# Key sums as running float32 sums instead of TensorE columns, merged masks also on GpSimd, and a new instruction order, in a four-layer attention kernel

## The chip, the cores and the metric

One core of a Trainium2 chip runs one program. The metric is device time in microseconds for one execution. The profile speaks of five engines: PE is TensorE's matmuls (PEld its weight loads), DVE is VectorE, ACT is ScalarE, POOL is GpSimd and SP is SyncE, which here only issues DMAs.

## The reference

Four attention layers in a row, each with a residual: linear attention (A), windowed softmax attention (B), A, B, on 2048 tokens of width 512, with 32 heads of 16.

```python
def _A_ref(x, wqkv, wo):                      # linear attention
    q, k, v = heads(x @ wqkv)                 # 32 heads of 16
    phi = lambda t: jnp.where(t > 0, t + 1, jnp.exp(t)) + 1e-6
    pq, pk = phi(q), phi(k)
    kv = jnp.einsum("bhsd,bhse->bhde", pk, v)
    z = jnp.einsum("bhsd->bhd", pk)           # the key sums
    num = jnp.einsum("bhqd,bhde->bhqe", pq, kv)
    den = jnp.einsum("bhqd,bhd->bhq", pq, z)[..., None] + 1e-6
    return merge(num / den) @ wo

def _B_ref(x, wqkv, wo):                      # causal window of 256
    scores = q @ k.T * 16 ** -0.5, masked to 0 <= i - j < 256
    return merge(softmax(scores) @ v) @ wo

x = x + _A_ref(_layernorm(x), A_wqkv, A_wo)
x = x + _B_ref(_layernorm(x), B_wqkv, B_wo)
x = x + _A_ref(_layernorm(x), A_wqkv, A_wo)
x = x + _B_ref(_layernorm(x), B_wqkv, B_wo)
```

## The kernel before

The 2048 tokens are 16 tiles (T) of 128. The residual stream `xres`, the normalised and transposed activations `XQ`, the keys `pk` and the values `vA` of all tiles stay in SBUF.

The program is first recorded as a graph of small steps (`Graph.add`), each with the engines it may run on, a key that once ordered it, the data it reads and writes, and its PSUM bank. `place` then reads from a packed `TABLE` the total order of all steps, the engine of each step that has a choice, and the bank of each PSUM tile. `synchronise` puts in the waits that this order needs. Each engine plays its steps in that order, so an instruction that waits holds up everything behind it on its engine. Two rules in these functions bear on GpSimd: each of its steps waits for the one before it, and a long GpSimd step waits for the last preceding wide VectorE step in the order (`WIDE`: the clamp `E1`, the normalisation `xn`, the masks `mk` and `mf`).

The stages, with the names used below:

- Keys of layer 1 (`layer_a_keys`): for each tile the layer norm (`stats`, `aggr`, `eps`, `pow`, `xn`, L367 to L371; `pow` is on GpSimd), a transpose `T` by PE or by DMA, the key projection `k` (L406), and `phi` of it: exponential `E` on ScalarE (L429), clamp `E1` (L430) and `phi` (L431) on VectorE. Then `g` (L481) adds up the Gram matrix of normalised tile and keys in four PSUM banks. When all tiles are done, `ge` (L395) copies it to SBUF and `gv` (L495) multiplies it by the value weights, which gives the key-value matrix `kv`.
- The key sums `z` of layer 1 (L504): for each tile and each quarter of the width, one matmul with the 128 x 128 keys as weights and one column of ones as data, 64 in all, added up in PSUM.
- `barrier`: `kvm` masks the key-value matrix (L523), `zs` spreads the key sums (L524), `M` multiplies by the output weights (L527), `den`, `rec`, `spread` and `pqd` make the denominators and scale the queries with their reciprocals (L543 to L563). `rec` and `pqd` are small SBUF tiles of these steps.
- The windowed layers (`middle`): per tile the linear layer's output `aout`, norm, projections `bq`, `bk`, `bv` (L406, L420) with copies `bqe`, `bke`, `bve` (L395, L591, L592), scores `s` (L638, and L679 or L682 for the far part) with exponentials `ex` (L648, L692), masks `mk` (L657, L658, L702) and `mf` (L710, L711), values `pv` (L731), division (L742, L743), a DMA transpose `oT` of the output tile and the output projection `bout`, then the residual (L574). In the first windowed layer a mask may be on VectorE or GpSimd, as `TABLE` says. In the second one, near and far masks of most tiles are merged, and this merged `mk` (L702) is a VectorE step only.
- In the second linear layer, keys and values are projected as tiles come out of the windowed layer. At its end `a_kv` adds up the key-value matrix of all tiles, and with each tile's four matmuls (L457) come its four key-sum matmuls (L460):

```python
for f in range(4):
    e.matmul(K.ps(kv)[:, fs], K.vA[:, t, fs], K.pk[:, t, fs], start=t == 0 and f == 0, stop=t == T - 1)
for f in range(4):
    m = e.matmul(K.ps(z)[:, f:f + 1], K.pk[:, t, fs], K.ones[:, 0:1], start=t == 0 and f == 0, stop=t == T - 1)
```

The table `oT` has room for two transposed output tiles, used in turn.

## Time and profile before

| | |
|---|---|
| time, median of 3 runs | 408.69 us (408.23 to 409.67) |
| profiled execution, own time | 409.79 us |
| its span | 408.1 us |
| granted TensorE clock, mean | 0.999 |

The profile follows that one execution. Busy times of engines overlap. The chain that ended last goes back from the last instruction, at each step to what released it. An idle time in square brackets is that of the engine just before the group, with what ended it.

### The profile page before, as it was taken

What the parts mean: (1) busy time and instruction counts of PE and PEld (TensorE: products, weight loads), DVE (VectorE), ACT (ScalarE), POOL (GpSimd) and SP (SyncE); (2) the same over time, 40 slices, a digit from 0 to 9 for tenths busy, and PEclk for the clock granted to TensorE, in tenths of its full rate; (3) what the DMA queues carried; (4) which work ended last, traced back from release to release, by engine and by line L of the source; (5) the groups of instructions that cost most, each with busy time, mean ns of one, the idle gap of its engine ahead of it and who ended that gap; (6) DMA issues with size and microseconds to landing.
All of it is one profiled execution on the core that took longest, in us unless ns stands there. A gap on an engine that the chain in (4) does not pass through costs nothing.

```text
span 408.1 us, 18068 instructions
## 1 busy us (share of the span) xinstructions
PE 386.1 (95%) x7922; PEld 262.9 (64%) x7997; DVE 333.4 (82%) x758; ACT 341.3 (84%) x441; POOL 151.6 (37%) x246
## 2 busy tenths in 40 slices
PE   8999999998999999999999999999999999899895
PEld 4544776766575566565665777676767766576663
DVE  5998898979998898887857789988798768776774
ACT  3465569998999999999998345999899999999992
POOL 3555624443464455451742223132313223030351
PEclk9999999999999999999999999999999999999999
DMA  7934316333263535343232000345214433345352
GB/s 247 243 65 103 106 41 136 106 77 85 69 95 81 120 83 113 75 116 93 60 72 41 16 2 27 98 100 126 65 46 121 109 89 74 74 111 115 83 146 81
DMA packets 67654, 37.88 MB, mean 93 GB/s; under 512 B 48248, under 2 KB 62712, under 8 KB 67576
## 3 DMA queue, kind: packets, MB, share of 16 engines
q1 hardware_dynamic: 67184, 35.67, 36.6%
q8 instruction: 63, 1.03, 1.1%
q0 software_dynamic: 384, 1.05, 0.7%
q14 instruction: 15, 0.12, 0.1%
q10 hardware_dynamic: 8, 0.00, 0.0%
HBM read 6.29 MB, written 2.10 MB: 21 GB/s over the span
## 4 chain that ended last, share of the span: by engine, by line
PE 69%; ACT 12%; DVE 9%; DMA 5%; issue 2%; SPq 1%; ACTq 0%
PE ps L406 22%; PE ps L420 18%; PE ps L731 14%; ACT pb L648 9%; PE ps L638 7%; DMA xres<-in_A_x_dram 2%; PE ps L682 2%; DMA pb<-in_B_wqkv_dram 2%; DVE stats L367 1%; DVE vp L431 1%; PE ps L679 1%; ACT vp L648 1%; PE ps L457 1%; ACT pb L692 1%; DVE o L743 1%
## 5 line engine op out<-in xcount | busy, mean ns | idle before, releaser
L648 ACT ACTIVATE pb<-ps 128x1024 bf16<-128x1024 f32 (+3 forms) x224 | 198.4, 973 | 8.1 <-PE ps L638 6.6
L731 PEld LDWEIGHTS ps<-vB,pb 128*128 128x128 bf16 x2560 | 77.7, 96 | 11.2 <-issue 5.0
L731 PE MATMUL ps<-vB,pb 128*128 128x34 bf16 x2560 | 83.1, 177 | 1.0 <-issue 0.8
L420 PE MATMUL ps<-xT,wBp 128*128 128x128 bf16 x1024 | 68.8, 219 | 0.3 <-ACT pb L648 0.3
L420 PEld LDWEIGHTS ps<-xT,wBp 128*128 128x128 bf16 x1024 | 58.7, 98 | 10.6 <-issue 4.6
L710 POOL TENSOR_SCALAR_AFFINE_SELECT pb<-pb 128x1024 bf16<-128x1024 bf16 x35 | 40.4, 1155 | 64.0 <-DVE pb L702 37.2
L429 ACT ACTIVATE tE<-ps 128x512 bf16<-128x512 f32 x64 | 37.8, 605 | 24.6 <-PE ps L406 15.0
L692 ACT ACTIVATE pb<-ps 128x1024 bf16<-128x1024 f32 x50 | 49.3, 1052 | 2.1 <-PE ps L682 1.0
L657 POOL TENSOR_SCALAR_AFFINE_SELECT pb<-pb 128x512 bf16<-128x512 bf16 x50 | 33.7, 674 | 45.0 <-ACT pb L648 18.1
L574 DVE TENSOR_TENSOR xres<-ps,xres 128x512 bf16<-128x512 f32 x63 | 42.8, 682 | 9.3 <-PE ps L406 9.0
L638 PE MATMUL ps<-XQ,kB 32*128 32x256 bf16 (+2 forms) x1024 | 48.1, 262 | 2.2 <-ACT pb L648 0.8
L370 POOL TENSOR_TENSOR rs<-ve,negh 128x1 f32<-128x1 f32 x64 | 37.0, 578 | 32.1 <-DVE ve L369 27.5
L406 PE MATMUL ps<-wA,XQ 128*128 128x512 bf16 x179 | 45.9, 379 | 2.8 <-DMA XQ<-vp 0.8
L367 DVE BATCH_NORM_STATS2 stats<-xres 128x6 f32<-128x512 bf16 x64 | 43.7, 685 | 3.1 <-DMA xres<-in_A_x_dram 2.3
L420 PE MATMUL ps<-XQ,wA 128*128 128x128 bf16 x512 | 35.4, 219 | 0.1
L369 POOL TENSOR_SCALAR ve<-mv 128x1 f32<-128x1 f32 x45 | 11.3, 252 | 63.2 <-DVE mv L368 61.1
L420 PEld LDWEIGHTS ps<-XQ,wA 128*128 128x128 bf16 x512 | 30.5, 98 | 5.9 <-issue 0.7
L638 PEld LDWEIGHTS ps<-XQ,kB 32*128 32x128 bf16 x1024 | 15.4, 92 | 27.6 <-ACT pb L648 9.3
L742 DVE RECIPROCAL rc<-ps 128x16 f32<-128x16 f32 x64 | 16.1, 252 | 20.2 <-PE ps L731 19.7
L406 PE MATMUL ps<-wBv,xT 128*128 128x512 bf16 x108 | 30.1, 380 | 2.4 <-issue 1.3
L406 PE MATMUL ps<-wBo,oT 128*128 128x512 bf16 x103 | 28.5, 380 | 3.0 <-issue 1.8
L406 PE MATMUL ps<-M,XQ 128*128 128x512 bf16 x114 | 29.7, 380 | 1.3 <-issue 0.6
(116 smaller groups left out, 562.0 us busy)
## 6 DMA issues: line engine op xcount, KB each, us to landing
vB<-vS SPq DMA_DIRECT2D x64, 136.0 KB, 2.6
kB<-vp SPq DMA_DIRECT2D x64, 128.0 KB, 2.4
wA<-in_A_wqkv_dram SPq DMA_DIRECT2D x3, 512.0 KB, 5.2
xres<-in_A_x_dram SPq DMA_DIRECT2D x2, 512.0 KB, 4.8
pb<-in_B_wqkv_dram SPq DMA_DIRECT2D x1, 1024.0 KB, 8.6
out_dram<-xres POOLq DMA_DIRECT2D x8, 128.0 KB, 2.7
out_dram<-xres SPq DMA_DIRECT2D x7, 128.0 KB, 2.9
xres<-in_A_x_dram SPq DMA_DIRECT2D x3, 256.0 KB, 4.9
```

Source lines behind the costliest of these rows:

```text
L367: self.on("DVE", "stats", lambda e: e.bn_stats(K.stats[:, t, :], K.xres[:, t, :]), key, dve(512), rd=[("xres", t)], wr=[("stats", t)])
L370: self.pow = self.on("POOL", "pow", lambda e: e.tensor_tensor(K.rs[:, t, :], K.ve[:, t, :], K.negh[:], ALU.pow), key + 0.03, (640, 690), r ...
L406: m = e.matmul(K.ps(ps), lhs(c), rhs(c), start=c == 0, stop=c == 3)
L420: m = e.matmul(K.ps(ps)[:, f * P:(f + 1) * P], w(c, f), xT(c), start=c == 0, stop=c == 3)
L429: self.on("ACT", "E", lambda e: e.activation(K.tE[:, s, :], K.ps(ps), ACT.Exp, bias=0.0), key, act(512), wr=[("tE", s)], ps=[ps])
L574: self.on("DVE", "res", lambda e: e.tensor_tensor(K.xres[:, t, :], K.ps(po), K.xres[:, t, :], ALU.add), key, dve(512), rd=[("xres", t)], w ...
L638: m = e.matmul(K.ps(ps[gq])[:, ns * i:ns * i + ns], K.kB[rows, j % 4, 2 * f + b, :, :], K.XQ[rows, f, q:q + ns], start=True, stop=True, ti ...
L648: return e.activation(out(h, ns).rearrange("p (f g) c -> p f g c", f=n), i, ACT.Exp, bias=0.0, scale=0.25)
L657: return e.affine_select(out=x, in_=x, compare_op=ALU.is_ge, fill=0.0, base=1, pattern=[[0, 4 * n], [2, 64]], channel_multiplier=-1)
L692: return e.activation(o.rearrange("p (f g) b c -> p f g b c", g=2), i, ACT.Exp, bias=0.0, scale=0.25)
L710: return e.affine_select(out=x, in_=x, compare_op=ALU.is_ge, fill=0.0, base=-2, pattern=[[0, 16], [-2, 64]], channel_multiplier=1)
L731: m = e.matmul(K.ps(ps)[:, 34 * u:34 * u + 34], K.P((b // 2) % rp)[:, f, gq % 2 * 2 + gq // 2, o:o + P], K.vB[:, (b // 2) % 4, b % 2, r, : ...
```

## The change

Four things change.

1. The key sums of 13 of the 16 tiles in each linear layer (`SUMMED`; the three left are tiles 13 to 15). Their keys are added into one float32 tile, one after the other (`za`, 12 adds of 128 x 512), each add on GpSimd or VectorE. The sum is then split into two bf16 parts: the high part `zh` is a rounded copy, the low part `zl` is the sum less the high part. Eight matmuls (`zp`) add both parts into the same PSUM columns as the plain key sums of the other three tiles. In each layer 52 key-sum matmuls go and 8 come. In both layers 9 adds are on GpSimd and 3 on VectorE; in the first, the high part is on ScalarE and the low part on VectorE, in the second both are on GpSimd. The float32 sum lies in the memory of `oT`, the parts in `pqd` and `rec`.
2. The transposed output of a windowed tile now goes to the tile's own columns of `XQ`, since `oT` is taken.
3. A merged mask may also be on GpSimd, as two selects instead of one VectorE multiplication. Of 56 merged masks, 40 are.
4. `TABLE` is new: another order of all steps, another choice of engine for many copies, masks and small steps, and other PSUM banks.

The diff also brings functions that are switched off (`SIDES = False` and `ALONE = T`): another form of the value matmuls, and query projections of two tiles at a time. Neither is built.

```diff
+SIDES = False
+ALONE = T
+SUMMED = [(p, t) for p in (1, 2) for t in range(13)]
...
     def a_kv(self, t, kv, z, key):
         K = self
+        alone = (2, t) not in SUMMED
...
-            for f in range(4):
+            for f in range(4 * alone):
                 fs = slice(f * P, (f + 1) * P)
-                m = e.matmul(K.ps(z)[:, f:f + 1], K.pk[:, t, fs], K.ones[:, 0:1], start=t == 0 and f == 0, stop=t == T - 1, skip_group_check=True)
+                m = e.matmul(K.ps(z)[:, f:f + 1], K.pk[:, t, fs], K.ones[:, 0:1], start=t == first and f == 0, stop=t == T - 1, skip_group_check=True)
...
+    def sum_rows(self, ph, z, key):
+        K = self
+        ts = [t for t in range(T) if (ph, t) in SUMMED]
+        acc = lambda: K.oT[:].rearrange("p a f n -> p (a f n)").bitcast(F32)
+        parts = [lambda: K.pqd[:].rearrange("p f n -> p (f n)"), lambda: K.rec[:].rearrange("p f n -> p (f n)")]
+        names = [[("pqd",)], [("rec", G) for G in range(4)]]
+        cost = {"POOL": (1090, 1150), "DVE": dve(512, "sum")}
+        for n in range(1, len(ts)):
+            x = (lambda: K.pk[:, ts[0], :]) if n == 1 else acc
+            self.g.add("za", cost, lambda e, eng, x=x, t=ts[n]: e.tensor_tensor(acc(), x(), K.pk[:, t, :], ALU.add), key - 0.02 * (len(ts) - n), rd=[("pk", ts[n])] + ([("pk", ts[0])] if n == 1 else [("sum",)]), wr=[("sum",)])
+        self.g.add("zh", {"POOL": (550, 613), "ACT": act(512)}, lambda e, eng: e.activation(parts[0](), acc(), ACT.Copy) if eng == "ACT" else e.tensor_copy(parts[0](), acc()), key, rd=[("sum",)], wr=names[0])
+        self.g.add("zl", cost, lambda e, eng: e.tensor_tensor(parts[1](), acc(), parts[0](), ALU.subtract), key, rd=[("sum",)] + names[0], wr=names[1])
+
+        def put(e):
+            m = None
+            for x in parts:
+                for f in range(4):
+                    m = e.matmul(K.ps(z)[:, f:f + 1], x()[:, f * P:(f + 1) * P], K.ones[:, 0:1], start=False, stop=True, skip_group_check=True)
+            return m
+
+        self.pe("zp", put, key + 0.1, 8, 1, rd=[("ones",)] + names[0] + names[1], ps=[z])
...
-                def mk(e, b=b, fs=fs):
+                def mk(e, eng, b=b, fs=fs):
...
+                    if eng == "POOL":
+                        for a in range(2):
+                            m = e.affine_select(out=o[:, :, a, :], in_=x[:, :, a, :], compare_op=ALU.is_ge, fill=0.0, base=1 + 64 * a, pattern=[[0, 8], [2, 32]], channel_multiplier=-1)
+                        return m
...
-                self.on("DVE", "mk", mk, ...
+                self.g.add("mk", {"DVE": dve(512, "2x"), "POOL": (780, 840)}, mk, ...
...
     def b_out(self, j, key, by_pe):
-        self.transpose("oT", lambda: K.o[:, s, :], lambda: K.oT[:, s, :, :], [("o", s, 0), ("o", s, 1)], [("oT", s)], key - 0.15, by_pe)
-        po = self.tok("bout", j, lambda f: K.oT[:, s, f, :], lambda f: K.wBo[:, f, :], [("oT", s), ("wBo",)], key)
+        oT = lambda: K.XQ[:, :, j * P:(j + 1) * P]
+        self.transpose("oT", lambda: K.o[:, s, :], oT, [("o", s, 0), ("o", s, 1)], [("XQ", j)], key - 0.15, by_pe)
+        po = self.tok("bout", j, lambda f: oT()[:, f, :], lambda f: K.wBo[:, f, :], [("XQ", j), ("wBo",)], key)
```

More of the change, by code (lines that the diff above doesn't have):

```diff
@@ L461, in put @@
             return m
[L463 removed]
+        first = min([x for x in range(T) if (2, x) not in SUMMED])
+        self.pe("kv", put, key, 4, 128, occ=330 if alone else 216, rd=[("pk", t), ("vA", t)] + [("ones",)] * alone, ps=[kv, z] if alone else [kv], after=self.closing)
+    def sum_rows(self, ph, z, key):
+        K = self
+        ts = [t for t in range(T) if (ph, t) in SUMMED]
[9 more added lines that the diff above has]
+        def put(e):
+            m = None
+            for x in parts:
+                for f in range(4):
+                    m = e.matmul(K.ps(z)[:, f:f + 1], x()[:, f * P:(f + 1) * P], K.ones[:, 0:1], start=False, stop=True, skip_group_check=True)
+            return m
+        self.pe("zp", put, key + 0.1, 8, 1, rd=[("ones",)] + names[0] + names[1], ps=[z])
```

220 lines of the change are left out of this document (153 added, 67 removed).

## The prediction, written before the changed kernel ran

> **What bounds the kernel now.** I read the page's busy shares and its chain first, then a table of stages, because a share of 408 us is a mean over stages with different limits.
>
> ```profile
> span 408.1 us, 18068 instructions
> PE 386.1 (95%) x7922; PEld 262.9 (64%) x7997; DVE 333.4 (82%) x758; ACT 341.3 (84%) x441; POOL 151.6 (37%) x246
> PE 69%; ACT 12%; DVE 9%; DMA 5%; issue 2%; SPq 1%; ACTq 0%
> ```
>
> TensorE is busy for 386.1 of 408.1 us and carries 69% of the chain that ended last. GpSimd, at 37%, is the engine with room. The stages (start and end, length, then busy us of each engine):
>
> ```profile
> 21.40:35.20 13.80, 13.75 (x87) 6.85 (x86) 13.77 (x39) 6.99 (x13) 7.99 (x21) 1.00 0.29 59
> 35.20:44.60 9.40, 9.20 (x102) 4.82 (x100) 7.44 (x15) 4.97 (x8) 6.12 (x10) 1.00 0.67 195
> 76.00:224.00 148.00, 142.10 (x3007) 95.35 (x3036) 123.06 (x277) 142.76 (x171) 68.12 (x101) 1.00 0.38 86
> 224.00:242.00 18.00, 17.78 (x335) 13.72 (x339) 14.30 (x32) 6.48 (x12) 2.89 (x6) 1.00 0.05 10
> 272.00:340.00 68.00, 65.15 (x1616) 46.13 (x1624) 54.99 (x125) 63.30 (x81) 16.94 (x20) 1.00 0.37 92
> 340.00:395.00 55.00, 50.28 (x1454) 36.22 (x1462) 40.29 (x94) 53.62 (x65) 15.16 (x19) 1.00 0.43 101
> ```
>
> The columns are PE, PEld, DVE, ACT, POOL, clock, DMA share, GB/s. Three kinds of stage show. The first keys (21.4 to 35.2) have PE and VectorE both full, 13.75 and 13.77 of 13.80. The turn from the first windowed layer to the second linear layer (224 to 242) is TensorE alone, 17.78 of 18.00. The windowed layers (76 to 224, 272 to 395) are ScalarE and TensorE together: ScalarE 142.76 of 148, and 53.62 of 55 at the end, while VectorE has 28 us free between 272 and 395. So matmuls taken out of a linear layer are worth their own time, work added to VectorE there may cost its own time, and in the windowed layers only ScalarE's work or a wait of PE or ScalarE counts.
>
> **Key sums of the first linear layer.** They stand at the end of the keys. The first rows are of the chain (start, us, what), the others of the timeline:
>
> ```profile
> 43.58 1.18 PE ps L504 x48
> 24.05 0.60 DVE stats L367
> 24.65 0.19 DVE tE L430
> 25.29 0.60 DVE vp L431
> 27.61 0.09 DVE mv L368
> ```
>
> ```profile
> 20.08 0.77 ACT L355 ACTIVATE wBp<-pb 128x512 bf16<-128x512 bf16 x1 [3.01 <-DMA pb<-in_B_wqkv_dram]
> 21.31 0.29 DVE L430 TENSOR_SCALAR tE<-tE 128x512 bf16<-128x512 bf16 x1 [1.37 <-ACT tE L429]
> 43.62 0.69 DVE L395 CAST kB<-ps 128x512 bf16<-128x512 f32 x1 [0.17 <-PE ps L481]
> 44.62 0.61 PE L495 MATMUL ps<-kB,wA 128*128 128x128 bf16 x8
> ```
>
> A key-sum matmul takes 1.18 / 48 = 0.0246 us of the chain. 52 of 64 go (13 tiles by 4), 8 come back for the two parts: 44 x 0.0246 = **-1.08 us**. This is not free of conditions: the 48 also fill the time in which the last copy of the Gram matrix (43.62, 0.69 long) is made, for which the matmuls of L495 wait until 44.62. The new order of PE puts two halves of a query projection (16 matmuls) and the first denominators in that place. That is work which stood later, so I take the whole 1.08; if the cover failed it would be 0.
>
> The new work stands on three engines. Of the 12 adds, 9 are on GpSimd and 3 on VectorE; ScalarE makes the high part, VectorE the low part. The last add, of tile 12, is ordered before the exponential of tile 15; the low part stands right behind the last keys' VectorE step (0.60 to 0.69), while PE still has two 512-column pairs of the Gram matrix and 12 plain key sums to do. I cost the two parts at nothing; with that cover gone, the low part would hold up PE, and the query projection queued behind it, by its own 0.6.
>
> **VectorE's chain in that layer.** By the chain's pitch a full VectorE pass over a tile is 0.60, the clamp 0.19, the small ones 0.09. A float32 add on VectorE is in no row; the nearest are the 0.60 passes (the clamp's 0.19 is the other end), and I take 0.60. Up to the last normalised tile, the new order has two clamps and two epsilons more: 2 x 0.19 + 2 x 0.09 = +0.56. From there to the last keys it has three adds more and three clamps fewer: 1.80 - 0.57 = +1.23. The stretch 35.2 to 44.6, in which those stand, has 9.40 - 7.44 = 1.96 us of VectorE idle, which hides the 1.23. Against the 0.56 stands a wait that goes: ScalarE's first weight copy sat 3.01 us on its DMA with exponentials queued behind it, and VectorE idled 1.37 for one of them. In the new order that copy stands two ScalarE instructions later, and VectorE has about 1.9 us more of other work ahead of the exponential behind it, more than the 1.37. Net 0.56 - 1.37 = -0.81 at best; the whole 1.79 exposed and no wait gone is +1.8. I take **-0.5**.
>
> **Price of a GpSimd add.** The trace has no two-input pass of 512 elements on GpSimd. Rows by form (busy, mean ns):
>
> ```profile
> L710 POOL TENSOR_SCALAR_AFFINE_SELECT pb<-pb 128x1024 bf16<-128x1024 bf16 x35 | 40.4, 1155 | 64.0 <-DVE pb L702 37.2 <-DVE vp L711 10.5 <-ACT pb L692 5.8
> L657 POOL TENSOR_SCALAR_AFFINE_SELECT pb<-pb 128x512 bf16<-128x512 bf16 x50 | 33.7, 674 | 45.0 <-ACT pb L648 18.1 <-DVE tE L430 8.3 <-DVE pb L658 7.7
> L702 DVE TENSOR_TENSOR pb<-pb,tri 128x512 bf16<-128x512 bf16 x44 | 17.3, 413 | 0.7 <-ACT pb L692 0.3
> L431 DVE SCALAR_TENSOR_TENSOR vp<-ps,tE 128x512 bf16<-128x512 f32 x32 | 21.7, 681 | 0.4
> L395 ACT ACTIVATE XQ<-ps 128x512 bf16<-128x512 f32 x10 | 6.0, 603 | 1.1 <-PE ps L420 0.7
> L395 ACT ACTIVATE vS<-ps 128x512 bf16<-128x512 f32 x8 | 5.5, 688 | 0.4 <-PE ps L406 0.3
> L591 ACT ACTIVATE vp<-ps 128x512 bf16<-128x512 f32 x6 | 4.5, 756 | 0.7 <-PE ps L420 0.7
> L548 ACT ACTIVATE rec<-recf 128x128 bf16<-128x128 f32 x6 | 1.9, 310 | 2.8 <-DVE recf L547 2.8
> ```
>
> 512 more elements cost 1155 - 674 = 481 ns, so 0.19 fixed and 0.94 ns an element. A second input that costs nothing gives 0.67, one that costs a second pass 0.674 + 0.481 = 1.16. I take 1.16, since nothing shows the second input to be free. [...] No run here shows such an add yet.
>
> **Key sums of the second linear layer.** Timeline:
>
> ```profile
> 229.08 0.38 PE L457 MATMUL ps<-vp 128*128 128x128 bf16 x4
> 229.30 0.24 PE L460 MATMUL ps<-ones,vp 128*128 128x1 bf16 x4
> 229.40 0.38 PE L457 MATMUL ps<-vp 128*128 128x128 bf16 x4
> ```
>
> Four key sums take 229.40 - 229.30 = 0.10 of PE; 13 tiles lose them: -1.30. Eight part sums add 0.20. Here both parts are GpSimd's, and the low part waits for tile 15's clamp although it doesn't read it (an ordering rule keeps GpSimd's long work behind VectorE's wide work). From the clamp, the low part takes 1.16; the other way, tile 15's keys and its four matmuls, takes 0.68 + 0.22 = 0.90. PE would wait 0.26 plus a hand-over: 0.35, between 0 (add at 0.67) and 0.9. Queued behind that wait on PE are a query half, the denominators and the output matrix, and VectorE's scaled sums wait for it. Sum: -1.30 + 0.20 + 0.35 = **-0.75**.
>
> **Windowed layers.** Matmuls and exponentials are the same in number. Counted between the first and the last exponential, ScalarE's other work changes. In the first windowed layer: two query copies (0.60) and a key copy (0.76) more, a windowed value copy (0.69), a linear-layer value copy (taken as 0.60 too) and a reciprocal copy (0.31) fewer: 1.20 + 0.76 - 0.69 - 0.60 - 0.31 = +0.36; ScalarE is 96% busy, so **+0.3**. In the second: a key copy more, two value copies, a query copy and a reciprocal copy fewer: 0.76 - 1.38 - 0.60 - 0.31 = -1.53. Of the 56 merged masks there, all on VectorE (L702), 40 go to GpSimd as two selects each. VectorE loses 40 x 0.413 = 16.5 us where it has 28 free; GpSimd gets 80 selects of 256 elements at 0.19 + 0.24 = 0.43, some 34 us, where it was busy 32 of 123. Since ScalarE is the fuller engine, I take two thirds of its 1.53, **-1.0**, and nothing for VectorE's relief. The cover for the slower masks (0.86 instead of 0.41) is the matmuls queued on PE between a tile's exponentials and its values. The transposed outputs now land in the tile's own query columns, whose readers are done by then: no wait added, 0. The tail swaps one copy between ScalarE and VectorE: 0.
>
> **Sum.** -1.08 - 0.5 - 0.75 + 0.3 - 1.0 = -3.03. The profiled execution took 409.79 us (span 408.1 and 1.69 around it), so its like would take 406.8. It lay 1.1 above the median 408.69 of the runs, so against those I forecast 408.69 - 3.0 = **405.7**. If every term falls well (-1.08, -0.81, no wait of PE: -1.10, windowed layers -2.0 in place of -0.7) it is 403.7; where the bad ends (no cover in the first layer, the chain's +1.8, PE's wait 0.9) use up over half of it, it is 407.4. That is its own range; all of them together leave the cases below.
>
> **Rivals.** *VectorE is held up in the first layer* (slower). GpSimd's adds run beside VectorE's clamps, and a clamp can be caught:
>
> ```profile
> L430 DVE TENSOR_SCALAR tE<-tE x64: 229/286/694, 11.5 to 297.4; 128x512 bf16<-128x512 bf16 x64
> ```
>
> The slowest took 694 against a median of 286, 0.41 more. If each of the 9 adds catches one VectorE pass on a chain with no slack, that is 3.7, with the 1.79 of added work less the 1.37 wait +4.1; in place of -0.5 the sum is +1.6: 410.3. It decides once that layer's VectorE chain grows by over 2.5 us. The median near the minimum speaks against it: collisions are rare now, and the ordering rule keeps them so. [...] Chance 0.12.
>
> *Masks come late* (slower). Each of the 40 masks is 0.45 longer, 18 us in all, and GpSimd's queue also holds the norm's power steps. If a quarter reaches TensorE or ScalarE, that is +4.5 in place of -1.0: 408.69 + 2.5 = 411.2. It decides at about a fifth, 3.2 of the 18. For it: the value matmuls read the masked tiles directly, and PE runs its queue in order. Against it: GpSimd stays near half busy. Chance 0.14.
>
> *VectorE's relief counts* (faster still). From 272 to 395 PE idles 7.6 us and ScalarE 6.1; if two thirds of the latter go besides the 1.53, the -1.0 becomes -5.6: 401.1. Chance 0.14.
>
> *Nothing comes of it*: key sums only filled the wait for the copies, the adds' waits eat the rest, the new orders even out: 408.5. Chance 0.10.
>
> **How the numbers follow.** The forecast has 0.50. A measurement of this kernel can tell about 0.3% (1.2 us) from no change. Faster: 0.50 + 0.14 = 0.64; same: 0.10; slower: 0.12 + 0.14 = 0.26. From 401.5 to 411.3 the range takes in the forecast, the unchanged case, the two slower rivals at their prices and the nearer half of the fast case; what lies outside, the farther halves, is under 2 in 10.
>
> **What would show it.** Right: 44 fewer one-column matmuls in each linear layer, adds near 1.16 on GpSimd, the matmuls of L495 starting near 44.62 - 1.08 - 0.5 = 43.0 us, a PE wait under 1 us ahead of the part sums at the second turn, PE's idle between 272 and 395 at or below 7.6. Wrong: VectorE clamps or norm steps well over their 0.3 to 0.4 between 10 and 36 us; value matmuls (L731 now) waiting on GpSimd for several us; a total over 407.5.

## The result and the profile after

The changed kernel takes 419.39 us (median of 6 runs, 417.55 to 420.15), against 408.78 (408.23 to 410.17) for the kernel before beside it: a ratio of 1.0249, with a 95% interval of 1.0222 to 1.0277. The forecast was 405.7. The profiled execution has a span of 417.1 us, against 408.1.

The page of the changed kernel, in the lines that answer to those of before, with the line of the instruction loads, which will be needed later:

```profile
span 417.1 us, 18025 instructions
...
PE 388.0 (93%) x7836; PEld 261.5 (63%) x7909; DVE 341.9 (82%) x737; ACT 344.9 (83%) x441; POOL 200.6 (48%) x335
...
q8 instruction: 62, 1.02, 1.1%
...
PE 50%; DVE 25%; ACT 19%; issue 3%; DMA 1%; POOL 0%; POOLq 0%; ACTq 0%
```

VectorE's part of the chain went from 9 to 25%. The stages of the windowed layers (columns as before):

```profile
76.00:224.00 148.00, 139.01 (x2888) 92.03 (x2916) 127.44 (x271) 140.78 (x162) 77.49 (x107) 1.00 0.40 86
272.00:340.00 68.00, 65.33 (x1631) 48.72 (x1641) 53.35 (x112) 62.24 (x78) 32.57 (x62) 1.00 0.37 87
340.00:395.00 55.00, 49.83 (x1408) 34.43 (x1413) 34.96 (x76) 53.08 (x64) 26.93 (x50) 1.00 0.46 103
```

Both TensorE and ScalarE are less busy than before from 76 to 224 us (139.01 for 142.10, 140.78 for 142.76; each trace misses some 75 matmul records): something is late for both. The first loss is in the first linear layer. The matmuls on the Gram matrix start here (source view of their line, ns min/median/max, then first and last start):

```profile
L547 PE MATMUL ps<-kB,wA x16: 219/219/230, 48.6 to 49.4; 128*128 128x128 bf16 x16
```

That is 48.6 us, where 44.62 stood before and 43.0 was forecast. VectorE's clamps and norm steps between 8 and 48 us, before and then after (groups by form: busy, mean ns):

```profile
L430 DVE TENSOR_SCALAR tE<-tE 128x512 bf16<-128x512 bf16 x22 | 6.4, 301 | 2.7 <-ACT tE L429 2.7
L371 DVE TENSOR_SCALAR vp<-xres,mv,rs 128x512 bf16<-128x512 bf16 x14 | 5.6, 398 | 0.0
```

```profile
L435 DVE TENSOR_SCALAR tE<-tE 128x512 bf16<-128x512 bf16 x22 | 8.4, 386 | 0.4 <-ACT tE L434 0.3
L376 DVE TENSOR_SCALAR vp<-xres,mv,rs 128x512 bf16<-128x512 bf16 x14 | 7.7, 555 | 0.0
L504 DVE TENSOR_TENSOR oT<-oT,vp 128x512 f32<-128x512 f32 x3 | 2.3, 781 | 0.0
L506 DVE TENSOR_TENSOR rec<-oT,pqd 128x512 bf16<-128x512 f32 x1 | 0.7, 681 | 0.0
```

The same 22 clamps and 14 norm steps take 4.1 us more (8.4 + 7.7 against 6.4 + 5.6), and three adds and the low part bring 3.0, on an engine that is now busy for 39.3 of these 40 us, where it was for 35.5. Single steps show how the 4.1 came about (timeline: start, us):

```profile
16.84 1.16 POOL L504 TENSOR_TENSOR oT<-vp 128x512 f32<-128x512 bf16 x1
17.39 0.75 DVE L435 TENSOR_SCALAR tE<-tE 128x512 bf16<-128x512 bf16 x1
18.43 1.16 POOL L504 TENSOR_TENSOR oT<-oT,vp 128x512 f32<-128x512 f32 x1
18.46 0.68 DVE L437 SCALAR_TENSOR_TENSOR vp<-ps,tE 128x512 bf16<-128x512 f32 x1
...
23.88 2.39 POOL L504 TENSOR_TENSOR oT<-oT,vp 128x512 f32<-128x512 f32 x2
25.20 1.22 DVE L435 TENSOR_SCALAR tE<-tE 128x512 bf16<-128x512 bf16 x1
```

The clamp at 17.39 falls into an add that runs from 16.84 to 18.00, and lasts until 18.14. The one at 25.20 falls into the second of two adds, which ends at 26.27, and lasts until 26.42, four times its usual length. Both end 0.15 us behind the add's end, and so do seven of the eight clamps and norm steps of this trace that were issued while an add ran (0.148 to 0.151 us). The eighth, issued 0.05 us behind the add's start, went first, and that add took 1.31. The VectorE step at 18.46, which reads PSUM, runs beside an add for its usual 0.68. In three of the traces with adds 12 statistics steps and 33 steps that read PSUM were issued while an add had 0.3 us or more to run; none was longer than usual, while most clamps and norm steps and both masks were (in the changed kernel a mask step of 0.42 took 1.26). In what follows, "hold-up" is by how much VectorE's clamps, norm steps, masks and adds exceed the median of their kind, counted where it is over 0.2 us: 2.3 us in the kernel before, 14.0 in the changed one, of which 4.7 lie in the first layer, 7.6 from 50 to 250 us and 1.8 behind.

### The profile page after: what moved, and what is told of

Same layout as the page of the kernel before. It is cut to its first block, busy times and chain, and to the rows that moved or that the text cites. A ratio compares the mean times of both kernels' runs of the same rounds, so it can differ in the third digit from the quotient of the medians.

```text
span 417.1 us, 18025 instructions
## 1 busy us (share of the span) xinstructions
PE 388.0 (93%) x7836; PEld 261.5 (63%) x7909; DVE 341.9 (82%) x737; ACT 344.9 (83%) x441; POOL 200.6 (48%) x335
## 3 DMA queue, kind: packets, MB, share of 16 engines
q8 instruction: 62, 1.02, 1.1%
## 4 chain that ended last, share of the span: by engine, by line
PE 50%; DVE 25%; ACT 19%; issue 3%; DMA 1%; POOL 0%; POOLq 0%; ACTq 0%
PE ps L411 16%; ACT pb L708 14%; PE ps L425 11%; PE ps L857 10%; PE ps L698 6%; DVE XQ L623 3%; DVE stats L372 3%; DVE tE L435 3%; ACT pb L752 3%; DVE vp L437 3%; DVE XQ L437 2%; DVE xres L634 2%; DVE vp L376 1%; PE ps L742 1%; ACT vp L708 1%
## 5 line engine op out<-in xcount | busy, mean ns | idle before, releaser
L857 PE MATMUL ps<-vB,pb 128*128 128x34 bf16 x2560 | 84.6, 177 | 3.1 <-issue 1.7
L375 POOL TENSOR_TENSOR rs<-ve,negh 128x1 f32<-128x1 f32 x64 | 37.1, 579 | 26.9 <-DVE ve L374 20.2
L774 POOL TENSOR_SCALAR_AFFINE_SELECT pb<-pb 128x1024 bf16<-128x1024 bf16 x32 | 37.6, 1176 | 16.4 <-DVE xn L376 8.3
L763 POOL TENSOR_SCALAR_AFFINE_SELECT pb<-pb 128x256 bf16<-128x256 bf16 x60 | 25.9, 456 | 24.9 <-ACT pb L708 8.1
L374 POOL TENSOR_SCALAR ve<-mv 128x1 f32<-128x1 f32 x43 | 10.4, 242 | 54.9 <-DVE mv L373 52.7
```

Of the source, the lines that this page charges most:

```text
L375: self.pow = self.on("POOL", "pow", lambda e: e.tensor_tensor(K.rs[:, t, :], K.ve[:, t, :], K.negh[:], ALU.pow), key + 0.03, (640, 690), r ...
L774: return e.affine_select(out=x, in_=x, compare_op=ALU.is_ge, fill=0.0, base=-2, pattern=[[0, 16], [-2, 64]], channel_multiplier=1)
L857: m = e.matmul(K.ps(ps)[:, 34 * u:34 * u + 34], K.P((b // 2) % rp)[:, f, gq % 2 * 2 + gq // 2, o:o + P], K.vB[:, (b // 2) % 4, b % 2, r, : ...
```

## Experiments: what each part costs

Four kernels beside the kernel before at 409.07. The first two cut the sums to one column, in both layers and in the first alone; the third also gives all key sums back to TensorE, so that the new order is left by itself; the fourth is the changed kernel with its 40 merged masks back on VectorE.

```diff
-e.tensor_tensor(acc(), x(), K.pk[:, t, :], ALU.add)
+e.tensor_tensor(acc()[:, 0:1], x()[:, 0:1], K.pk[:, t, 0:1], ALU.add)
```

> The changed kernel with its adds, its high part and its low part cut to one column in both linear layers (so 13 tiles are missing from the key sums); order, engines, waits and matmuls unchanged. Theory A, the adds themselves cost the time (GpSimd's adds hold VectorE's clamps and norm steps, and VectorE's adds stand on a full chain): most of the 10.6 us come back, 409 to 412. Theory B, the new order is slower whatever it carries: 417 to 419. Theory C, the masks on GpSimd cost it: 417 to 419.

> The same cut in the first linear layer only. Theory A with the loss in the first layer and carried on: 3.5 to 4.5 us come back, about 415.5, the rest stays with the second layer's adds, which run beside the first windowed layer. If those cost nothing, this equals the run with no adds at all. Theories B and C: 418 to 420.

```diff
-for x in parts:
+for t in ts:
...
-        m = e.matmul(K.ps(z)[:, f:f + 1], x()[:, f * P:(f + 1) * P], K.ones[:, 0:1], ...)
+        m = e.matmul(K.ps(z)[:, f:f + 1], K.pk[:, t, f * P:(f + 1) * P], K.ones[:, 0:1], ...)
```

> The changed kernel's order, engines and masks, adds cut to one column, and all 64 key sums of each linear layer back on TensorE (52 of them in one go where the part sums stood); the result is the full one. Against the run with no adds it costs 44 matmuls of 0.0246 us in each layer, +2.2 us. Theory A: 411 to 414, a little over the kernel before. Theory B: 419 to 421.

```diff
+if o.name == "mk" and o.merged:
+    o.eng = "DVE"
```

> The changed kernel with its 40 GpSimd merged masks back on VectorE at the same places of the order; adds unchanged. Theory C, the masks in two selects on GpSimd cost the time: 3 us or more come back, under 416.5. Theories A and B: between 418 and 421, since ScalarE and TensorE bound that layer and VectorE has room.

Measured: both layers' adds cut 413.47 (ratio 1.0120, 1.0075 to 1.0166), the first layer's alone 413.60 (1.0120, 1.0083 to 1.0158), the order alone 415.49 (1.0164, 1.0116 to 1.0212), masks on VectorE 435.48 (1.0644, 1.0596 to 1.0692). So the first layer's adds are worth 419.39 - 413.60 = 5.8 us (5.3 by the ratios), the second layer's 0.1, and the order by itself loses 6.4. The 2.0 between the third and the first would be the key sums' saving; their programs differ in length, and what that can do is shown below, but in the traces the kernel with the sums given back falls behind by 1.1 us at the end of each linear layer (starts of ScalarE's activations compared one by one), which is the saving at its place. These parts add up: 6.4 - 2.0 + 0.1 + 5.8 = 10.3. Within the new order the masks on GpSimd are worth 16 us: it was laid out for them. Up to 8.5 of these, an estimate, are the clock's: with the masks on VectorE it stood at 0.50 for 17.1 us in the profiled execution, and half of that is 8.5.

## Experiments: the hold-up in the first layer

First the 9 GpSimd adds of this layer were cut into four pieces of 128 columns; then, in another kernel, they were set behind the VectorE steps that they had held up.

```diff
+for c in range(0, 512, 128):
+    m = e.tensor_tensor(acc()[:, c:c + 128], x()[:, c:c + 128], K.pk[:, t, c:c + 128], ALU.add)
```

> The changed kernel with one edit: each of the first linear layer's 9 adds on GpSimd is issued as four pieces of 128 columns (36 instructions in place of 9; the 3 adds on VectorE and everything of the second layer stay whole). The sums and all results are unchanged. Theory A (a clamp or norm step of VectorE that is issued while a GpSimd instruction runs waits until that instruction has ended; after that it runs): a caught step is held up by at most one piece, some 0.3 us, instead of up to 1.16, so of the 4.1 us that the clamps and norm steps gained (clamps 6.62 to 8.48, norm steps 5.58 to 7.77 us in the first layer's stretch) most goes, unless VectorE falls behind again on the next piece: 1.5 to 4 us faster than the changed kernel's 419.39, so 415.5 to 418, longest clamp and norm step under 0.75 us. Rival B (the two engines share a path's rate, and a step is slowed in proportion to the time it overlaps): the same number of columns is added in the same time, so the clamps and norm steps keep their sum of 16 us and the time stays at 419.4 or rises by the fixed cost of 27 more instructions on GpSimd. Rival C (the loss is VectorE's own three adds and the low-part subtraction, 3.0 us, not the held-up steps): no change, 419.4.

```diff
+MOVED = [([106, 110], 119), ([156], 172), ([202], 211), ([203, 204], 219), ([242], 258), ([299, 300], 301)]
+for what, behind in MOVED:          # the steps at these places go behind that place
```

> The changed kernel with its GpSimd instructions of the first linear layer set behind the VectorE steps that they held up there: 8 adds and 2 constants move by 2 to 17 places in the order, so that a clamp or norm step of VectorE goes first and the add waits for it; all adds, engines and sums as in the change. Theory A (each held-up step delays VectorE's unbroken chain of this layer by what it loses): of the 4.7 us of hold-up in the first layer some 3 to 4 go, and the time falls from 419.39 by 2 to 4 us, to 415.5 to 417.5. Rival B (the adds' own chain ends the layer: moved back, the last add, its parts and the matmuls on them come later by as much): no gain, 419 to 420. Rival C (the hold-up comes back at other steps, since VectorE is busy without a gap and each add must run beside some step): hold-up still 3 us or more, 418 to 419.4.

The groups of the kernel with quarters, the source view of its adds, and the groups of the kernel with the adds set behind:

```profile
L435 DVE TENSOR_SCALAR tE<-tE 128x512 bf16<-128x512 bf16 x22 | 7.7, 356 | 0.0
L376 DVE TENSOR_SCALAR vp<-xres,mv,rs 128x512 bf16<-128x512 bf16 x14 | 6.3, 459 | 1.5 <-POOL rs L375 1.4
```

```profile
L506 POOL TENSOR_TENSOR oT<-oT,vp x40: 418/427/1213, 18.9 to 243.9; 128x128 f32<-128x128 f32 x32, 128x512 f32<-128x512 f32 x8
```

```profile
L443 DVE TENSOR_SCALAR tE<-tE 128x512 bf16<-128x512 bf16 x22 | 7.2, 332 | 0.2 <-ACT tE L442 0.2
L384 DVE TENSOR_SCALAR vp<-xres,mv,rs 128x512 bf16<-128x512 bf16 x14 | 6.1, 439 | 0.6 <-POOL rs L383 0.5
```

With quarters the longest clamp held up by an add fell from 1.22 to 0.50 and the longest norm step from 1.25 to 0.62, and half of the 4.1 us went: a held-up step waited for the instruction that was running, not for a share of a rate (the nine caught with 0.2 us or more of a piece to run end 0.15 us behind that piece). But a piece takes 0.427, four of them 1.71 in place of 1.16, GpSimd's norm steps (L375) queue behind them, and VectorE now waits 1.4 us for these: 417.82 (1.0221, 1.0200 to 1.0241), hardly a gain. Set behind, the adds cost 1.9 us less: 417.53 (1.0216, 1.0194 to 1.0239), hold-up in the layer 1.9 in place of 4.7. Both intervals still overlap with that of the changed kernel. The layer, from the start of its first norm step to that of its first scaled query, lasts 42.0 us before, 46.5 after, 45.4 with the adds set behind and 42.2 with this layer's adds cut: its adds lose 4.3 us here and 0.6 right behind, which stay lost to the end. That held-up steps are not the whole of it shows in the adds set behind: 2.8 us of hold-up went, but the layer got only 1.1 shorter, as VectorE now waited 0.7 us for a moved add and 0.5 for a late `pow`. No run parts the hold-up from VectorE's own 3.0 us of adds and low part.

## Experiments: the second layer's sums on the old order

The old order was kept, and 11 adds on GpSimd, its two parts and their 8 matmuls were put into it for the second layer. The first kernel has each add 15 places behind the step that finishes its tile; the second has it where VectorE's trace has no clamp, norm or mask step for 1.2 us; the third is the first with adds of one column.

```diff
+SUMS = 12
...
+        at = last + (15 if n_.name == "za" else 1)
+    order.insert(at, n_)
```

> The kernel before, its order kept, with key sums taken off TensorE in the second linear layer only: tiles 0 to 11 are added in float32 by GpSimd (11 adds of 1.16 us, each put in 15 places behind the step that finishes its tile), split by GpSimd into two bf16 parts, and added by 8 matmuls of one column; 48 of the 64 one-column matmuls go. The transposed attention output goes to the query tile's place, as in the change, so that its old buffer holds the sums. First linear layer, masks and all results as before. Theory A (the second layer's part of the change is a gain of its own: 48 x 0.0246 = 1.18 us less TensorE work between the windowed layer and the sums, less 8 x 0.0246 = 0.20 for the parts, the adds hidden in a stretch where VectorE has room): 0.5 to 1.2 us faster than the kernel before, 407.5 to 408.3. Rival B (GpSimd's adds hold up VectorE's clamps and norm steps here too, and its own masks and norm constants queue behind them): slower by 1 to 4 us, 410 to 413. Rival C (the stretch is set by the last tile's query and key steps and not by the key sums): within 0.5 us of before.

```diff
-        at = last + (15 if n_.name == "za" else 1)
+PLACES = [718, 842, 900, 979, 1112, 1175, 1238, 1259, 1357, 1382, 1445, 1520, 1520]
+for n_, at in zip(new, PLACES):
+    order.insert(order.index(plain[at]), n_)
```

> The same 11 adds, two parts and 48 key-sum matmuls saved as in the second layer put on the old order by itself (413.85 against 409.01 for the kernel before), but every add is put where the trace of the kernel before shows VectorE without a clamp, norm or mask step for at least 1.2 us and GpSimd free. There, 7 norm steps had grown from 0.32 to 0.41 us to between 0.58 and 1.33, 5.1 us in all, as an add was running when they were issued. Theory A (those held-up steps are the whole loss): norm steps back near 0.41 us, and the gain of the key sums is left: 0.3 to 1.2 us faster than the kernel before, 407.8 to 408.7. Rival B (the loss came with the moved transposed output or with the adds' and parts' place behind the window's last tile): still 3 to 5 us slower, 412 to 414.

```diff
-e.tensor_tensor(acc(), x(), K.pk[:, t, :], ALU.add)
+e.tensor_tensor(acc()[:, 0:1], x()[:, 0:1], K.pk[:, t, 0:1], ALU.add)
```

> The second layer's sums on the old order at their first places (behind the step that finishes each tile; 413.85 us), with one edit: each add and each of the two parts works on one column of 512, so the sum it gives leaves the other columns out; instructions, waits, matmuls and the place of the transposed output are the same. Theory A (the loss of 4.8 us is GpSimd instructions of 1.16 us that hold up norm steps): an add of one column is over in 0.1 us or so, nothing is held up, and the time is that of the kernel before less the key sums, 407.8 to 409. Rival B (the moved transposed output, or the queue of GpSimd with 13 more entries, is what costs): 412 to 414, little changed.

Norm steps from 100 to 220 us in the kernel before, the first and the second:

```profile
L371 DVE TENSOR_SCALAR xn<-xres,mv,rs 128x512 bf16<-128x512 bf16 x19 | 7.8, 409 | 0.3 <-POOL rs L370 0.3
```

```profile
L383 DVE TENSOR_SCALAR xn<-xres,mv,rs 128x512 bf16<-128x512 bf16 x19 | 12.9, 677 | 1.2 <-POOL rs L382 1.2
```

```profile
L383 DVE TENSOR_SCALAR xn<-xres,mv,rs 128x512 bf16<-128x512 bf16 x19 | 7.8, 411 | 0.4 <-POOL rs L382 0.4
```

The first is 4.8 us slower than before, 413.85 against 409.01 (1.0119, 1.0103 to 1.0135), with 5.1 us of hold-up in seven norm steps. Placed with the trace at hand, the same instructions cost 0.7 us: 409.07 against 408.35 (1.0019, 1.0002 to 1.0036). One column: 409.19 (1.0020, 1.0004 to 1.0035). So here hold-ups of norm steps reach the end nearly in full (4.8 of 5.1 us), even in a windowed layer where VectorE has room; a norm step heads the transfer and the projections of its tile. And with no hold-up left, the 48 key-sum matmuls saved still bring no gain.

## Experiments: masks and the windowed layers

The 40 masks alone on the old order; and the changed kernel with every GpSimd step that held up VectorE, masks too, set behind it.

```diff
+if o.name == "mk" and len(o.emit.__defaults__ or ()) == 2:   # a merged mask
+    near += 1
+    o.eng = "POOL" if near - 1 in MASKS else "DVE"
```

> The kernel before, with its order and its key sums on TensorE untouched; only the 40 merged window masks that the change gave to GpSimd are given to it here too, each as two selects, at the places in the order where VectorE did them. Theory A (moving masks is no cost in itself; VectorE and GpSimd both have room in the windowed layers, and the loss of 6.4 us of the new order without sums lies in the order): within 2 us of the kernel before, 407 to 411. Rival B (the masks are what costs: two selects of about 0.45 us take the place of one VectorE instruction of 0.47, arrive 0.5 us later, and the value matmuls behind them wait; 40 masks, of which perhaps 15 are waited for by 0.4 us): 3 to 7 us slower, 412 to 416. Rival C (the masks are worth what their return to VectorE cost in the new order, 16 us): several us faster than the kernel before, under 405.

```diff
-MOVED = [..., ([242], 258), ([299, 300], 301)]
+MOVED = [..., ([242], 258), ([299, 300], 301), ([620], 625), ([621], 631), ([902], 907), ([976], 988), ...]
```

> As the last one, and in the windowed layers too: 17 GpSimd masks and 2 adds of the second sums set behind the VectorE step that they held up in the changed kernel's trace (held-up time there: 4.7 us in the first layer, 7.6 us from 50 to 250 us, 1.8 us behind; in the kernel before 0.4, 1.5 and 0.4). Theory A (held-up VectorE steps, not the masks' engine or the key sums, are what the new order loses by): hold-up in all below 6 us, and the time falls by at least 5 us from 419.39, to 411 to 414.5. Rival B (the new order loses by other waits, such as the transposing transfers and the masks that the value matmuls wait for; masks put back by 0.5 to 1 us then come later still): the gain stays that of the first layer or less, 416 to 420.

The masks on the old order: 413.03 (1.0093, 1.0072 to 1.0113). Against the kernel before, next to nothing is lost until 310 us, 1.3 us from there to 384 and 2.8 behind. TensorE's waits from 380 to 396 us (us, times, longest), and the stretches behind, show the last part:

```profile
PE ps L742 <- POOL pb L710: 1.4, 1, 1.4
```

```profile
394.00:394.50 0.50, 0.50 (x25) 0.42 (x21) 0.06 (x1) 0.00 (x0) 0.43 (x2) 1.00 0.50 105
394.50:395.00 0.50, 0.50 (x9) 0.13 (x2) 0.47 (x2) 0.22 (x1) 0.42 (x1) 0.50 0.00 0
...
397.00:397.50 0.50, 0.50 (x6) 0.19 (x3) 0.50 (x2) 0.34 (x1) 0.00 (x0) 0.50 0.00 0
397.50:398.00 0.50, 0.50 (x3) 0.22 (x2) 0.12 (x1) 0.50 (x1) 0.00 (x0) 0.59 0.41 84
398.00:398.50 0.50, 0.50 (x10) 0.27 (x8) 0.00 (x0) 0.50 (x2) 0.00 (x0) 1.00 0.88 178
```

Value matmuls wait 1.4 us for a merged mask, until 393.0; 1.5 us later the granted clock (third column from the end) falls to 0.50 and stays there until 397.9: by estimate up to half of these 3.4 us, 1.7, is lost to TensorE's work. The one run of this kernel with a mean clock of 0.999 took 411.43. Not every such wait is followed by a fall: one of 1.5 us at 159.5 in the order alone was not. Setting the masks back was a miss: 426.22 (1.0434, 1.0414 to 1.0453). Hold-up fell from 14.0 to 4.6 us, but up to 190 us nothing was won over the kernel with only the adds set behind, and then masks came too late for the value matmuls (timeline, the idle time before them in brackets):

```profile
208.22 1.47 PE L865 MATMUL ps<-vB,pb 128*128 128x34 bf16 x48 [3.76 <-POOL pb L782]
...
211.42 0.75 PE L865 MATMUL ps<-vB,pb 128*128 128x34 bf16 x20 [1.19 <-POOL pb L725]
```

Behind these waits the clock stood at 0.50 for 10.2 us, by estimate up to half of it, 5.1 us, more. So what the hold-ups in the windowed layers cost stays open: taking them away this way brought larger waits, and up to 190 us their absence won nothing.

## Experiments: the order, and what a saved matmul is worth

TensorE from 52 to 245 us, in the old order with only the outputs' place changed, and in the new order alone:

```profile
52.00:245.00 193.00, 191.22 (x3755) 127.21 (x3753) 163.12 (x360) 170.77 (x212) 82.43 (x128) 1.00 0.35 78
```

```profile
52.00:245.00 193.00, 186.09 (x3654) 122.55 (x3652) 162.59 (x356) 168.70 (x206) 82.86 (x134) 1.00 0.36 78
```

In the old order TensorE hardly ever stands still there (191.22 of 193), in the new one for 6.9 us. From the first scaled query to the second layer's masked key-value matrix (`kvm`) the old order takes 192.3 us and the new one 197.2; so 4.9 of its loss lie here, in the first windowed layer and the second keys. So four groups of matmuls that waited there were moved behind the next ones that were ready, and in another kernel the kernel before got the outputs' new place alone.

```diff
+MOVED = [([453], 455), ([913, 917, 918], 920), ([1175], 1177), ([1348, 1353], 1355)]
```

> The new order alone (all key sums on TensorE, the adds cut to one column; 415.49 us against 409.07 for the kernel before), with four instructions groups of TensorE moved by a few places. Between 52 and 245 us TensorE stood still for 6.6 us there, against 1.7 us in the old order (with 40 masks moved, the same up to 255 us); the gaps over 0.5 us are five: 0.64 at 64.4 (value projection, its bank not yet copied), 1.13 at 134.5 (query projection, the transposing transfer of its tile has not landed), 1.50 at 159.5 (output projection, a transfer again), 0.78 at 177.4 (key projection, bank) and 0.52 at 206.4 (value projection, bank). Here the waiting group goes behind the next group that is ready at all but the one at 159.5, where nothing is ready. Theory A (these gaps are the order's loss in this stretch): 2 to 3 us less than the order alone, 412.5 to 413.7. Rival B (TensorE is fed by ScalarE and VectorE at their own pace there; a gap filled opens again behind): within 1 us of the order alone, 414.5 to 416.5.

```diff
-po = self.tok("bout", j, lambda f: K.oT[:, s, f, :], ..., [("oT", s), ("wBo",)], key)
+oT = lambda: K.XQ[:, :, j * P:(j + 1) * P]
+po = self.tok("bout", j, lambda f: oT()[:, f, :], ..., [("XQ", j), ("wBo",)], key)
```

> The kernel before with one edit: the transposed attention output of the windowed layers goes to the query tile's place instead of a buffer of its own, as in the change; nothing else. Theory A (the place is free: the tile has long been read): within 0.3% of the kernel before, 407.5 to 409.5. Rival B (the place costs what the 48 saved key-sum matmuls were worth, as both kernels with them on the old order came out level): 0.7 to 1.5 us slower, 409 to 410.

Mended: 415.22 (1.0158, 1.0134 to 1.0182) against 415.49; the gaps were filled and opened again some places on, 6.6 us in all. The place alone is free: 408.43 against 408.79 (0.9995, 0.9977 to 1.0014).

Then key-sum matmuls were left out of the kernel before, or added, with its order kept:

```diff
-    for f in range(4):                          # second layer, at each tile t
+    for f in range(4 * (t >= 13)):
...
-    for t in range(4 * q, 4 * q + 4):           # first layer, in four groups q
-        for f in range(4):
+    for t in range(13, 16) if q == 3 else [None]:
+        for f in range(4) if q == 3 else [q]:
```

> The kernel before with key-sum matmuls left out and nothing in their place: 49 of the first linear layer's 64 and 52 of the second's 64, so the key sums hold 3 tiles of 16 (and one column each of others). It is the most that the change could gain on TensorE in the old order. Theory A (TensorE ends both stretches, and a one-column matmul is worth its 0.0246 us): 101 x 0.0246 = 2.5 us faster, 405.5 to 406.7. Rival B (other work ends one or both of them): 0 to 1.2 us faster, 407 to 408.4.

The first of these two edits alone, and the second alone:

> The kernel before with 52 of the 64 key-sum matmuls of the second linear layer left out and nothing in their place, so that layer's key sums hold 3 tiles of 16; the first layer and all that runs before 225 us as before. Theory A (those matmuls stand on TensorE's path, and nothing before them is moved): 52 x 0.0246 = 1.3 us faster than the kernel before, 407.0 to 408.2. Rival B (the second windowed layer, started 1.3 us earlier, runs into new waits as the first one did when its start moved): 1 to 5 us slower, 410 to 414.

> The kernel before with 49 of the 64 key-sum matmuls of the first linear layer left out and nothing in their place (its key sums hold 3 tiles of 16 and a column each of others); the second layer as before. Theory A (the first layer's end comes 0.4 us earlier or so, the transfers of the first windowed layer are issued at other times, some of the issues of transposing transfers take 2.1 to 2.5 us in place of 1.19 at places where TensorE waits for them, and the time so lost is kept): 412 to 415.5, TensorE idle for over 5 us between 52 and 245 us. Rival B (a saving is a saving): 0.4 to 1.2 us faster, 407.2 to 408.5.

```diff
+if q == 3:                                      # a second time, into unused columns
+    m = e.matmul(K.ps(z)[:, 4 + f:5 + f], K.pk[:, t, f * P:(f + 1) * P], K.ones[:, 0:1], ...)
```

> The kernel before with 16 more one-column matmuls: the last four tiles' key sums of the first linear layer are also added into four columns that nobody reads, 16 x 0.0246 = 0.4 us of TensorE right ahead of that layer's end. All results as before. Theory A (any shift of the layer's end sets the windowed layer's waits off): 411 to 415, TensorE idle for over 4 us between 52 and 245 us. Rival B (a later end is harmless, as everything behind it shifts along with its transfers): 0.2 to 0.6 us slower, 408.9 to 409.5.

```diff
+for _ in range(2 * (q < 3)):                    # beside the second edit above
+    m = e.matmul(K.ps(z)[:, 16:464], K.ones[:], K.pk[:, 13, 0:448], start=False, stop=False, ...)
```

> The kernel with 49 key-sum matmuls left out in the first linear layer (its key sums hold 3 tiles of 16), and at the three places where 15 of them stood each, two matmuls of 448 columns into columns that nobody reads, about 0.19 us each, 1.1 us in all: the layer's end comes back to where it is in the kernel before, and TensorE's program stays 43 instructions shorter. Theory A (the earlier end of the layer sets off the waits of the windowed layer): back to 408 to 409.3, TensorE idle for under 2.5 us between 52 and 245 us. Rival B (not the time but the shorter program changes what happens behind): 412.5 to 416, idle for over 4.5 us there, as with the matmuls left out.

Measured: 101 fewer 414.06 against 408.79 (1.0129, 1.0097 to 1.0161); 52 fewer in the second layer 408.75 against 408.39 (1.0016, 0.9998 to 1.0035); 49 fewer in the first 414.86 (1.0183, 1.0151 to 1.0216); 16 more in the first 408.43 (1.0007, 0.9992 to 1.0022); 49 fewer with six longer ones in their place 414.46 against 408.22 (1.0148, 1.0123 to 1.0172). Leaving work out of the first layer made the kernel 6 us slower; leaving it out of the second, or adding some, changed nothing that the runs can tell. The stretch with 16 more, and with 49 fewer, and behind the latter the waits of TensorE's weight loads in it:

```profile
52.00:245.00 193.00, 191.22 (x3758) 127.39 (x3757) 163.16 (x360) 171.23 (x212) 82.46 (x128) 1.00 0.34 78
```

```profile
52.00:245.00 193.00, 187.38 (x3698) 123.88 (x3694) 158.35 (x351) 167.65 (x206) 80.46 (x126) 1.00 0.35 78
```

```profile
PEld ps L406 <- DMA oT<-o: 1.7, 3, 0.6
PEld ps L420 <- DMA xT<-xn: 1.2, 2, 1.0
PEld ps L406 <- DMA XQ<-xn: 0.9, 1, 0.9
```

TensorE waits for transposing transfers (its matmuls, which overlap the weight loads, for 2.3 of the 5.6 us that they stand still), which it does not do at all with 16 more. The issue of these transfers on SP's queue is longer at some places. The same one with 101 fewer and with 16 more (timeline), and between them the first one's instruction queue from 55.2 to 57.5:

```profile
55.27 2.12 SPq L377 DMA_TRANSPOSE xT<-xn  x1
```

```profile
q8 instruction: 1, 0.02, 2.9%
```

```profile
55.81 1.21 SPq L377 DMA_TRANSPOSE xT<-xn  x1
```

In the first, a load of 16 KB of program falls into the issue (queue q8 of the page, which lists 62 of them, 1.02 MB, in the changed kernel); in the second none does. Over the 20 traces with 73 such issues each behind 50 us, 217 took over 1.5 us (up to 2.8), and in every one such a load was under way; of the 1101 that took up to 1.3, 895 had none. The waits above come behind issues of the usual length, though (seven transfers, 1.19 to 1.30): there it is the landing that is late, 3.6 to 4.3 us after the issue, each time with a load that begins 0.7 to 2.1 us after the issue. Of all these transfers, the 842 with no load beginning within 2.4 us of their issue landed 2.48 us after it in the median, the 585 with one 3.80. The first such wait, with 49 fewer (DMA view from 73.1 to 76.7 us) and at the same transfer with 16 more (73.9 to 76.4; issue to landing in us at the end of the line):

```profile
q8 instruction: 1, 0.02, 2.2%
xT<-xn SPq DMA_TRANSPOSE x1, 3.6
```

```profile
xT<-xn SPq DMA_TRANSPOSE x1, 2.5
```

Up to this transfer the two kernels run the same course, the one with 49 fewer 0.8 us ahead; it then loses these 0.8 us to this one wait. So the loss begins with a load that falls on a transfer, not with the layer's earlier end. With the shorter program of TensorE the loads come at 64.7 and 73.8 us, with the longer one at 69.4 and 77.5.

This shows how the leaving-out comes to cost time at all, not each of its 6 us: 2.3 are waits for transfers. The kernel with six longer matmuls was meant to part the earlier end of the layer from the shorter program and did not: the longer matmuls ran in time that was idle, and the layer ended as early as without them. It stays open too why the new order's gaps refill; only two of its five large ones end with a transposing transfer.

## Why the prediction was wrong, and where it was right

- **VectorE's chain in the first layer, -0.5 (ends -0.81 and +1.8): the step that failed first.** The layer lost 4.3 us by its adds. The prediction put held-up steps at nothing in its sum, since collisions were rare and the ordering rule would keep them so; that rule makes GpSimd wait for VectorE, never the reverse. The rival "VectorE is held up" had the mechanism and the sign, its mark (clamps and norm steps well over 0.3 to 0.4 between 10 and 36 us) came true, and its +4.1 for the layer is near the 4.3. That its amount came so near is in part luck: it counted nine catches of 0.41, from the one caught clamp of the kernel before (0.694 us at 39.58, ending 0.15 behind a GpSimd select), which is 3.7; measured are seven, of 0.17 to 0.94, 3.9 in all. The seven waited until the add had ended (0.148 to 0.151 us behind it), so the price was set by what was left of the add's 1.16.
- **An add on VectorE at 0.60:** 0.688 (median of 6), up to 0.974. **An add on GpSimd at 1.16:** right, 1.159, as the tile view has it (ns min/median/max).

```profile
L504 POOL TENSOR_TENSOR oT<-oT,vp x16: 1153/1159/1312, 18.4 to 243.3; 128x512 f32<-128x512 f32 x16
L504 DVE TENSOR_TENSOR oT<-oT,vp x6: 676/688/974, 39.7 to 158.6; 128x512 f32<-128x512 f32 x6
```

- **First layer's key sums, -1.08:** right in size within the new order, where other work stands in their place: with them given back, that layer ends 1.1 us later. In the old order the saving is not to be had: from the last keys' VectorE step to the first matmul of L495 it takes 3.24 us with the outputs' place alone, 3.03 with 49 sums left out and 3.65 with 16 more. There, with the sums left out, TensorE waits 0.5 us for the last Gram copy, the condition that the prediction named.
- **Second layer, -0.75:** the wait of 0.35 on the low part did not come (the part sums follow the last plain ones without a gap), and the saving came, 1.1 in the new order. In the old order 52 sums left out are worth 0 (interval -0.1 to +1.4 us): the layer ended 0.6 us earlier, and that was lost again behind it.
- **Windowed layers, +0.3 and -1.0: the largest failure,** +6.4 for the order by itself, some 4.9 of it between the first scaled query and the second layer's `kvm`. Counting ScalarE's copies says nothing on when they are due; the waits that a new order brings stood in no term. Why its gaps open is not shown. The page also misled: 75 of 7997 matmul records are missing from it, and TensorE's idle time of 5.9 us from 76 to 224 us is 1.8 in the complete trace of the kernel with the outputs' place alone. So there was little for another order to win.
- **Masks to GpSimd, 0:** 4.0 us on the old order, where of the 2.8 lost behind 384 us one wait of 1.4 and 3.4 us at a clock of 0.50 (up to 1.7 by estimate) can account for all; the rival "Masks come late" has its mechanism there. In the new order it cannot be told apart. **The outputs' place, 0:** right.

## What to carry to other kernels

Before work is given to GpSimd, list the VectorE steps that it can hold up (here clamps of 0.28 us, norm steps of 0.41, masks of 0.42 and adds of 0.69, which took up to 1.24, 1.25, 1.35 and 0.97, not the 33 steps that read PSUM) and that will be issued while it runs: those held up in the changed kernel ended 0.14 to 0.54 us behind the GpSimd instruction, so what counts is where a long one is put, and with a trace at hand it can be put where it costs little. A total order that keeps TensorE busy to 99% is worth keeping (here 6.4 us, against 2.0 for the 88 matmuls saved); cost a new one by the waits of its own trace, not by sums of busy time, and try the saving by itself (leave the work out) before building what replaces it. Read a busy share with the number of records beside it.

## What the runs showed of the hardware that was not expected

- A VectorE clamp or norm step that is issued while a GpSimd float32 add runs ends 0.15 us behind the add's end (seven of eight in the changed kernel); 12 statistics steps and 33 steps that read PSUM, issued beside an add, were not held up.
- An issue of a transposing transfer on SP's queue took 1.19 to 1.3 us in 1101 of 1460 cases, and 1.5 to 2.8 in 217, in each of which a 16 KB load of program ran; the transfer landed 3.80 us after its issue in place of 2.48 (medians) where a load began in the first 2.4 us. With 49 one-column matmuls fewer on TensorE the loads fell elsewhere (64.7 and 73.8 us in place of 69.4 and 77.5), and the kernel took 6.5 us longer.
- A GpSimd add in float32 took 0.427 us for 128 columns and 1.159 for 512 (medians): by estimate from these two 0.18 fixed and 1.9 ns a column, so 0.18 for one column, where 0.1 was expected.
- One wait of TensorE of 1.4 us was followed, 1.5 us behind its end, by 3.4 us at a granted clock of 0.50. In the six traces with such a fall ahead of the end that miss no matmul record, TensorE had been idle for 0.8 to 2.3 us of a stretch as long as this fall (3.41, from 394.50 to 397.91) before each.
